# Sixteen transposes of the value tile moved from TensorE to the DMA, with a new start and a new order, in a fused scan and feed-forward kernel

## The chip, the cores and the metric

The kernel runs on one core of a Trainium2 chip. Times are device microseconds (us) of that core. A run is called slow when it takes over 1.5% more than the fastest run of the same kernel; ratios use the other runs ("fast runs") alone. The kernel before takes 269.89 us (median of 3 runs, 268.21 to 270.97).

## The reference, cut to what matters

```python
# r, k, v, w, a, b: [4 batches, 8 heads, 768 tokens, 40], float32
for t in range(S):
    y[:, :, t] = einsum('bhd,bhde->bhe', rt, state)
    Sa = einsum('bhde,bhe->bhd', state, at)
    state = state * wt[..., None, :] - einsum('bhd,bhe->bhde', Sa, bt)
    state = state + einsum('bhd,bhe->bhde', vt, kt)
x = y.transpose(0, 2, 1, 3).reshape(3072, 320)
out = maximum(x @ w_in, 0) ** 2 @ w_out        # w_in 320 x 2048, w_out 2048 x 320
```

A recurrence over 768 tokens in 32 independent heads gives `x`, and a feed-forward layer turns `x` into the output of 3072 rows of 320 floats.

## The kernel before

The scan is done in chunks of 64 tokens. Two batches at a time make a *group*: 12 chunks by 2 pairs of batches are 24 groups. Each group runs the recurrence of one chunk (KB, A, EB, XV, COR, ST) and the readout (CP, YC). Then its 128 rows go through the feed-forward layer (U, RL, SQ, D) and are stored (OE, OST). All operations of all groups stand in one long string, ORDER, which a search has produced; each engine is given its work in that order. `~10` in it means ten warm-up matmuls, whose result is not used.

Two parts matter here. The first is the value tile VM. After the correction (COR) two copies (MA, MB) finish VM; TensorE then transposes it in eight pieces (VT), VectorE copies the result out of PSUM (VTE), and CP reads it:

```python
def f():
    p = psum("vt", g, BF16)
    for i in range(8):
        nc.tensor.transpose(out=p[:, 128*i:128*i + 128], in_=vm[:, 128*i:128*i + 128], identity=ID[:])
add("VT", g, "PE", 0.447, f, [("MA", g), ("MB", g)], mode="M", alloc=("S", "vt"))
def f():
    nc.vector.tensor_copy(out=vmt[:], in_=psum("vt", g, BF16)[:])
add("VTE", g, "DVE", 0.692, f, [("VT", g), ("CP", g - 2)], frees="vt")
add("CP", g, "PE", 0.243, lambda: tri("cp", vmt, rh), [("VTE", g), ("RTE", g)], ...)
```

The second is the key tile KB. From group 6 on (`KDMA = 6`) it is transposed by one DMA already, issued on SP (KX), while groups 0 to 5 use TensorE (KT) and VectorE (KTE):

```python
nc.sync.dma_start_transpose(out=V(kbt, 0, [(128, 8), (1, 128)]), in_=kb[:])     # KX
```

The store of the group's result takes 128 partitions of 320 floats. Its rows lie in two batches of the output, and so its destination has an outermost dimension of 2:

```python
dst = out[b0 * T + c * L:b0 * T + c * L + L, :]
dst = bass.AP(dst.tensor, dst.offset, [[T * DM, 2], [DM, L], [1, DM]])   # 2 x 64 x 320
nc.sync.dma_start(out=dst, in_=osb[:])                                    # OST, once per group
```

Of the kernel before, what the change touches and what calls it, by code (L numbers as in the profile page):

```python
# [8 lines left out]
BF16 = mybir.dt.bfloat16  # L9
# [6 lines left out]
TBL.0 zK2.0 LWb.0 zL1.0 zR1.0 zS2.0 LWa.0 zV3.0 zR2.0 zU0.0 LKa.0 LWa.1 zA1.0 zS1.0 LKb.0 LWa.2 zF1.0 LBa.0 ones.0  # L16
zV1.0 UI.0 LAa.0 zF0.0 UE.0 LBb.0 ID.0 LWb.1 zL0.0 zF2.0 LN.0 LV1.0 SELB.0 LKb.1 TI.0 LO.0 zK0.0 LAb.0 zA0.0 zS0.0
LV0.0 ~10 CS.0 TE.0 LWb.2 zR0.0 EXN.0 I2.0 CE.0 LR.0 LAb.1 KBS1.0 KBS0.0 EXE.0 LAb.2 LN.1 zV0.0 ~3 KT.0 LR.1 LBa.1
AS.0 KTE.0 SEL.0 ~3 AT.0 wi1.0 LAa.1 MASK.0 LN.2 ATE.0 GLM.0 VC.0 LO.1 ~2 EB.0 LBb.1 EBE.0 LV0.1 ~1 CE.1 LKa.1 LO.2
EXE.1 zU1.0 LWb.3 ~1 XV.0 zK1.0 RT.0 LR.2 UB.0 zF3.0 LAa.2 LV1.1 UA.0 zV2.0 RTE.0 ~2 COR.0 wi2.0 CS.1 MA.0 LWa.3  # L20
CE.2 AS.1 MB.0 EXN.1 LKb.2 LV1.2 ~1 AT.1 VT.0 EXE.2 LAa.3 ATE.1 wj1.0 VTE.0 ST.0 KBS0.1 KBS1.1 CP.0 zR3.0 LBa.2
LV0.2 CPE.0 KT.1 LBb.2 wj2.0 LN.3 KTE.1 LKa.2 AS.2 ~2 CS.2 RT.1 EXN.2 STE.0 LAb.3 YC.0 wj0.0 RTE.1 EB.1 YE.0 LO.3
SX.0 VC.1 EBE.1 LKa.3 LR.3 CE.3 wi0.0 EXE.3 SXE.0 XV.1 LBa.3 LV1.3 wp0.0 AT.2 UA.1 RT.2 ATE.2 LKb.3 UB.1 KBS0.2 CS.3
wp1.0 RTE.2 COR.1 KBS1.2 LBb.3 XT.0 AS.3 MA.1 KT.2 XTE.0 MB.1 U1.0 wo0.0 KTE.2 EXN.3 VT.1 LV0.3 AT.3 VC.2 VTE.1 EB.2
UX1.0 GLM.1 GLM.2 EBE.2 UY1.0 LWb.4 ST.1 RL1.0 KBS0.3 LWa.4 STE.1 XV.2 X0.2 CP.1 LBb.4 UB.2 GLM.3 U0.0 CPE.1 KBS1.3
UA.2 UY0.0 LWa.5 UX0.0 wo1.0 KT.3 RL0.0 ATE.3 COR.2 KTE.3 YC.1 MA.2 YE.1 RT.3 MB.2 EB.3 SQ0.0 SX.1 RTE.3 LWb.5 XT.1
VT.2 XTE.1 LN.4 LKb.4 D0.0 EBE.3 VC.3 LO.4 ST.2 U0.1 LV0.4 SXE.1 CS.4 SQ1.0 D1.0 EXN.4 LAa.4 LBa.4 UX0.1 STE.2 LR.4
UY0.1 CE.4 VTE.2 RL0.1 LKa.4 XV.3 X0.3 CP.2 LWa.6 LN.5 U1.1 CPE.2 KBS1.4 UY1.1 EXE.4 LWa.7 UX1.1 UB.3 LAb.4 SX.2
LKb.5 RL1.1 SQ0.1 D2.0 LV1.4 SXE.2 D3.0 LWb.8 UA.3 LO.5 YC.2 OE.0 YS.2 LWb.6 KBS0.4 COR.3 YE.2 RT.4 LBa.7 D0.1 SQ1.1
RTE.4 LR.5 KT.4 LWb.7 MA.3 LV1.5 XT.2 D1.1 MB.3 XTE.2 AS.4 KTE.4 ST.3 LKa.5 VC.4 CS.5 LAb.5 U1.2 LBa.5 AT.4 LN.6  # L30
LAa.5 UX1.2 ATE.4 LBb.5 EXN.5 VT.3 LR.6 UY1.2 VTE.3 LV0.6 EB.4 RL1.2 OST.0 CE.5 EBE.4 LO.6 D2.1 LKa.7 EXE.5 LV0.5
RT.5 LN.7 STE.3 LBb.6 XV.4 KBS0.5 X0.4 U0.2 UB.4 CP.3 UA.4 D3.1 LAa.6 CPE.3 UX0.2 LKb.6 OE.1 KBS1.5 UY0.2 RTE.5
SQ1.2 SX.3 LAb.6 RL0.2 KT.5 LKa.6 SXE.3 CS.6 GLM.4 KTE.5 LBa.6 LO.7 COR.4 EXN.6 YC.3 SQ0.2 YS.3 LWa.8 AS.5 RT.6 MA.4
CS.7 YE.3 RTE.6 OST.1 D0.2 LV1.6 EXN.7 AT.5 XT.3 LWa.9 LV1.7 D1.2 ATE.5 VC.5 XTE.3 KBS1.6 EB.5 LKb.7 U0.3 MB.4 EBE.5
CE.6 LR.7 LWb.9 VT.4 LN.8 KBS0.6 D2.2 VTE.4 EXE.6 LBb.8 XV.5 LAa.7 X0.5 CP.4 UA.5 AS.6 D3.2 CPE.4 LBb.7 UB.5 UY0.3
OE.2 LO.8 KX.6 AT.6 VC.6 UX0.3 ATE.6 GLM.5 ST.4 LAb.7 RL0.3 YC.4 LKb.8 YS.4 LAb.8 COR.5 YE.4 CS.8 MA.5 LV1.8 U1.3
SQ0.3 LKa.9 MB.5 XT.4 UX1.3 KBS0.7 EXN.8 STE.4 UY1.3 VT.5 OST.2 LAa.8 RL1.3 XTE.4 D0.3 LWb.10 VTE.5 KBS1.7 EB.6
LBa.9 U0.4 SQ1.3 CE.7 LR.8 EBE.6 UY0.4 LN.9 LKb.9 UX0.4 EXE.7 LAb.9 D1.3 RL0.4 LWa.10 LO.9 SX.4 CP.5 SXE.4 GLM.6
ST.5 LV0.7 CPE.5 KX.7 RT.7 XV.6 AS.7 X0.6 D2.3 UA.6 SQ0.4 LV0.9 LKa.8 UB.6 D3.3 RTE.7 STE.5 U1.4 LR.9 LBa.8 CS.9
OE.3 LV1.9 COR.6 YC.5 MA.6 YS.5 LV0.8 UY1.4 YE.5 MB.6 UX1.4 KBS1.8 LKb.11 XT.5 SX.5 RL1.4 XTE.5 LKb.10 AT.7 SXE.5  # L40
CE.8 OST.3 SQ1.4 D0.4 EXE.8 VT.6 EXN.9 ATE.7 D1.4 LBb.9 LN.10 ST.6 VC.7 LO.10 LKa.11 U0.5 STE.6 EB.7 KBS0.8 LWb.11
UX0.5 EBE.7 D2.4 GLM.7 UY0.5 LAa.9 D3.4 VTE.6 RL0.5 KX.8 AS.8 RT.8 XV.7 LV0.10 X0.7 OE.4 SQ0.5 CP.6 U1.5 UA.7 OST.4
UY1.5 CPE.6 RTE.8 LWa.11 UX1.5 UB.7 AT.8 D0.5 RL1.5 ATE.8 SX.6 CS.10 SXE.6 LBb.12 YC.6 EXN.10 SQ1.5 COR.7 LWa.12
KBS0.9 YS.6 RT.9 MA.7 YE.6 D1.5 LWb.12 RTE.9 LAa.10 XT.6 D2.5 LBa.10 VC.8 XTE.6 KBS1.9 EB.8 MB.7 U0.6 EBE.8 LKa.10
LR.10 UY0.6 VT.7 GLM.8 LBb.10 LV1.10 UX0.6 VTE.7 D3.5 RL0.6 CE.9 KX.9 XV.8 OE.5 SQ0.6 X0.8 ST.7 EXE.9 CP.7 LN.11
STE.7 AS.9 OST.5 U1.6 UA.8 UY1.6 CPE.7 UB.8 LAb.10 UX1.6 LBb.11 D0.6 RL1.6 LO.11 AT.9 SX.7 ATE.9 LAb.11 LBa.11 CS.11
SQ1.6 LV1.11 YC.7 LWa.13 COR.8 YS.7 LV0.11 MA.8 D1.6 LWb.13 YE.7 MB.8 D2.6 LR.11 EXN.11 LWa.14 XT.7 KBS0.10 CE.10
XTE.7 VC.9 SXE.7 EB.9 U0.7 KBS1.10 EXE.10 EBE.9 ST.8 VC.10 VT.8 LAa.11 KX.10 UY0.7 LN.12 STE.8 D3.6 LV0.12 VTE.8
UX0.7 OE.6 AS.10 LWb.14 SX.8 RL0.7 RT.10 OST.6 SXE.8 LO.12 XV.9 X0.9 CP.8 UA.9 GLM.10 U1.7 LV1.12 CPE.8 RTE.10 UY1.7
UX1.7 LKb.14 UB.9 AT.10 RL1.7 LKb.12 CS.12 ATE.10 YC.8 SQ0.7 COR.9 LKa.12 KBS1.11 YS.8 RT.11 MA.9 YE.8 LBa.12 D0.7  # L50
EXN.12 KBS0.11 SQ1.7 XT.8 D1.7 MB.9 XTE.8 LAa.12 EB.10 LKb.13 VC.12 U0.8 EBE.10 GLM.9 UY0.8 LR.12 RTE.11 KX.11 UX0.8
CE.11 VT.9 LN.13 LBb.14 D2.7 VTE.9 EXE.11 LO.13 XV.10 RL0.8 LBb.13 X0.10 AS.11 ST.9 CP.9 STE.9 VC.11 U1.8 LAb.13
D3.7 UA.10 CPE.9 LAb.12 UY1.8 UB.10 SX.9 OE.7 LR.13 UX1.8 SQ0.8 OST.7 CS.13 RL1.8 LKa.14 SXE.9 YC.9 YS.9 COR.10
KBS1.12 LKa.13 YE.9 EXN.13 AT.11 D0.8 ATE.11 KBS0.12 MA.10 CE.12 XT.9 D1.8 LN.14 LAa.13 XTE.9 MB.10 SQ1.8 EB.11
LO.14 U0.9 EXE.12 UY0.9 EBE.11 KX.12 GLM.11 VT.10 LV1.13 UX0.9 LR.14 VTE.10 ST.10 LWa.15 AS.12 XV.11 STE.10 X0.11
LWa.16 CP.10 UB.11 D2.8 CPE.10 UA.11 AT.12 RL0.9 D3.8 LWb.15 COR.11 ATE.12 RT.12 LBa.13 MA.11 YC.10 YS.10 MB.11 U1.9
YE.10 CS.14 LKa.15 OE.8 SQ0.9 SX.10 EXN.14 OST.8 XT.10 UY1.9 XTE.10 UX1.9 LBa.15 VT.11 RL1.9 LBa.14 D0.9 KBS0.13
VTE.11 EB.12 LKa.16 U0.10 SQ1.9 LAa.14 CE.13 EBE.12 D1.9 LAb.14 EXE.13 LKb.15 UY0.10 LN.15 LV0.13 LWb.16 UX0.10
RTE.12 SXE.10 D2.9 KBS1.13 RL0.10 ST.11 AS.13 KX.13 XV.12 STE.11 X0.12 CP.11 UA.12 GLM.12 U1.10 LV0.15 CPE.11 D3.9
LBb.15 AT.13 LV1.14 OE.9 UY1.10 UB.12 ATE.13 UX1.10 OST.9 LO.15 SQ0.10 RT.13 RL1.10 COR.12 YC.11 LWb.18 YS.11  # L60
KBS0.14 CS.15 YE.11 RTE.13 D0.10 LWa.17 EXN.15 LAa.15 XT.11 SX.11 LBa.16 XTE.11 MA.12 KBS1.14 EB.13 U0.11 MB.12
EBE.13 CE.14 LV0.14 LWb.17 D1.10 LN.16 LAb.15 VT.12 SQ1.10 EXE.14 KX.14 UX0.11 VC.13 LO.16 VTE.12 UY0.11 LV1.15
D2.10 SXE.11 LKb.17 RL0.11 XV.13 AS.14 RT.14 LBb.16 ST.12 LR.15 X0.13 STE.12 U1.11 UA.13 CP.12 LR.16 UB.13 UY1.11
CPE.12 LV1.16 RTE.14 D3.10 UX1.11 OE.10 AT.14 SQ0.11 RL1.11 OST.10 YC.12 COR.13 ATE.14 KBS0.15 YS.12 LWa.18 CS.16
YE.12 MA.13 SX.12 LBb.17 LAa.16 SQ1.11 MB.13 CE.15 VC.15 LKb.16 LAb.16 VT.13 D0.11 VC.14 VTE.13 LV0.16 D1.11 EXE.15
SXE.12 XT.12 EXN.16 GLM.15 D2.11 XTE.12 AS.15 RT.15 U0.12 GLM.13 RTE.15 EB.14 KBS1.15 UY0.12 EBE.14 UX0.12 KX.15
AT.15 RL0.12 D3.11 XV.14 LBb.18 ST.13 OE.11 SQ0.12 X0.14 LN.17 OST.11 CP.13 U1.12 UA.14 LV1.17 CPE.13 D0.12 VC.16
UY1.12 LO.17 UB.14 UX1.12 LWa.19 ATE.15 LV0.17 STE.13 CS.17 RL1.12 LWb.20 YC.13 LR.17 YS.13 COR.14 LBa.17 YE.13
KBS0.16 D1.12 MA.14 LBa.18 XT.13 MB.14 CE.16 GLM.14 XTE.13 EXN.17 VT.14 LBa.19 EXE.16 ST.14 VTE.14 LN.18 U0.13 EB.15
SQ1.12 LR.18 UX0.13 LKa.17 LO.18 UY0.13 EBE.15 D2.12 LKb.18 RL0.13 KBS1.16 SX.13 STE.14 CP.14 LAb.17 KX.16 U1.13  # L70
CPE.14 XV.15 LV0.18 X0.15 RT.16 UA.15 D3.12 LAa.17 UB.15 SXE.13 UY1.13 RTE.16 LWb.19 AS.16 SQ0.13 COR.15 OE.12 YC.14
YS.14 LV1.18 MA.15 OST.12 CS.18 YE.14 UX1.13 MB.15 KBS0.17 AT.16 RL1.13 D0.13 ATE.16 LBb.19 KBS1.17 XT.14 SX.14
XTE.14 EXN.18 LKa.18 CE.17 ST.15 LWa.20 EXE.17 EB.16 AS.17 STE.15 U0.14 LWb.21 VT.15 SQ1.13 UX0.14 LKb.19 UY0.14
EBE.16 D1.13 RL0.14 SX.15 KX.17 D2.13 VTE.15 LN.19 D3.13 SXE.14 LR.19 LKb.20 XV.16 SXE.15 OE.13 LO.19 X0.16 RT.17
# [69 lines left out]
def kernel(  # L144
# [9 lines left out]
    moe_w_out: bass.AP,  # L154
    out: bass.AP,
):
    nc = tc.nc
    NB, NH, T, D = r.shape
    L = 64
    KDMA = 6  # L160
    AQ = 4
    NCH = T // L
    NG = NCH * (NB // 2)
    DFF = moe_w_in.shape[1]
    DM = moe_w_in.shape[0]

# [526 lines left out]
```

## Time and profile before

The profiled run of before took 264.9 us.

| engine | busy us | share |
|---|---|---|
| TensorE | 243.5 | 92% |
| VectorE | 180.1 | 68% |
| ScalarE | 163.2 | 62% |
| GpSimd | 162.3 | 61% |
| DMA (mean of 16 engines) | | 79% |

The prediction below shows and reads the lines of the page, the stretches and the chain of waits.

### The profile page before, as it was taken

What the parts mean: (1) busy time and instruction counts of PE and PEld (TensorE: products, weight loads), DVE (VectorE), ACT (ScalarE), POOL (GpSimd) and SP (SyncE); (2) the same over time, 40 slices, a digit from 0 to 9 for tenths busy, and PEclk for the clock granted to TensorE, in tenths of its full rate; (3) what the DMA queues carried; (4) which work ended last, traced back from release to release, by engine and by line L of the source; (5) the groups of instructions that cost most, each with busy time, mean ns of one, the idle gap of its engine ahead of it and who ended that gap; (6) DMA issues with size and microseconds to landing.
All of it is one profiled execution on the core that took longest, in us unless ns stands there. A gap on an engine that the chain in (4) does not pass through costs nothing.

```text
span 264.9 us, 13096 instructions
## 1 busy us (share of the span) xinstructions
PE 243.5 (92%) x5809; PEld 193.8 (73%) x5809; DVE 180.1 (68%) x296; ACT 163.2 (62%) x289; POOL 162.3 (61%) x244
## 2 busy tenths in 40 slices
PE   4887979999999999999999999999999899999970
PEld 1345767877877788787877788888878688878750
DVE  7659976696856676768666668686767658786520
ACT  2344665687755757775675876578485675646340
POOL 3789728987975469567489758576967593400000
PEclk9979999999999999999999999999999999999997
DMA  7999999798799699789699879779899677200110
GB/s 117 156 180 169 202 199 167 137 155 155 141 143 136 127 132 161 145 141 144 106 135 152 169 120 169 131 133 139 138 113 142 110 131 102 66 25 16 32 36 26
DMA packets 111913, 33.75 MB, mean 127 GB/s; under 512 B 101232, under 2 KB 109808, under 8 KB 111856
## 3 DMA queue, kind: packets, MB, share of 16 engines
q1 hardware_dynamic: 100272, 20.79, 52.0%
q0 software_dynamic: 9472, 11.80, 25.2%
q8 instruction: 45, 0.74, 1.2%
q10 hardware_dynamic: 2112, 0.33, 0.8%
q14 instruction: 12, 0.10, 0.1%
HBM read 28.84 MB, written 3.93 MB: 124 GB/s over the span
## 4 chain that ended last, share of the span: by engine, by line
PE 74%; DMA 5%; ACT 2%; issue 2%; POOL 1%; DVE 0%; ACTq 0%; POOLq 0%
PE fo L569 19%; PE hp L551 15%; DMA KBT<-KB 5%; PE hp L542 4%; PE vt L488 4%; PE sx L476 3%; PE eb L405 2%; PE cs L298 2%; PE x L420 2%; PE cp L405 2%; PE y L502 2%; PE ce L311 2%; PE rt L376 2%; PE st L457 2%; PE x L442 2%; PE ar L369 2%
## 5 line engine op out<-in xcount | busy, mean ns | idle before, releaser
L556 ACT ACTIVATE RL<-hp 128x1024 bf16<-128x1024 f32 x46 | 47.1, 1023 | 32.7 <-PE hp L551 32.2
L569 PE MATMUL fo<-WOUT,GT 128*128 128x320 bf16 x384 | 65.5, 300 | 0.6 <-DVE GT L560 0.5
L331 POOL TENSOR_TENSOR KB<-KBf,EXN 128x320 bf16<-128x320 f32 x45 | 40.6, 909 | 36.9 <-PE y L502 21.4
L551 PE MATMUL hp<-XT,WIN 128*128 128x128 bf16 x736 | 51.7, 219 | 1.1 <-issue 1.0
L551 PEld LDWEIGHTS <-WIN 128*128 128x128 bf16 x768 | 44.9, 98 | 4.8 <-issue 1.7
L560 DVE TENSOR_TENSOR GT<-RL 128x1024 bf16<-128x1024 bf16 x48 | 37.8, 787 | 9.0 <-ACT RL L556 8.9
L569 PEld LDWEIGHTS <-GT 128*128 128x128 bf16 x384 | 33.0, 98 | 11.9 <-DVE GT L560 1.1
L409 DVE TENSOR_TENSOR CPM<-cp,MASK 128x1024 bf16<-128x1024 f32 x24 | 29.3, 1220 | 8.5 <-PE cp L405 8.5
L409 DVE TENSOR_TENSOR EBM<-eb,MASK 128x1024 bf16<-128x1024 f32 x24 | 29.3, 1221 | 7.6 <-PE eb L405 7.4
L343 POOL DMA_DIRECT2D Vf<-in_v_dram x48 | 33.9, 706 | 0.0
L290 POOL TENSOR_TENSOR LLO<-LNW 128x320 bf16<-128x320 f32 x24 | 18.4, 767 | 19.5 <-ACT LNW L282 15.2
L264 POOL DMA_DIRECT2D Af<-in_a_dram x40 | 28.2, 706 | 0.4 <-issue 0.4
L433 ACT ACTIVATE UZ<-x 64x320 bf16<-64x320 f32 x48 | 20.7, 431 | 9.7 <-PE x L428 8.1
L337 POOL TENSOR_TENSOR A<-Af,EXE 128x320 bf16<-128x320 f32 x24 | 21.2, 882 | 6.8 <-ACT EXE L320 2.3
L447 ACT ACTIVATE VM<-x 64x320 bf16<-64x320 f32 x48 | 20.6, 430 | 7.6 <-PE x L442 6.8
L304 ACT ACTIVATE EXN<-cs 128x640 f32<-128x640 f32 x24 | 16.9, 702 | 10.4 <-PE cs L298 8.7
L468 DVE TENSOR_TENSOR STB<-st,GLM 128x640 bf16<-128x640 f32 x22 | 18.0, 818 | 7.7 <-PE st L462 7.1
L515 DVE TENSOR_TENSOR YB<-y,EXE 128x320 bf16<-128x320 f32 x24 | 11.8, 490 | 13.5 <-PE y L510 12.0
L492 DVE COPY VMT<-vt 128x1024 bf16<-128x1024 bf16 x24 | 16.5, 686 | 4.4 <-PE vt L488 4.3
L282 ACT ACTIVATE LNW<-Wf 128x320 f32<-128x320 f32 x24 | 11.2, 468 | 12.8 <-PE ce L315 7.0
L542 PE MATMUL hp<-XT,WIN 64*128 64x128 bf16 x368 | 18.1, 217 | 0.0
L347 ACT ACTIVATE VM<-Vf 128x640 bf16<-128x640 f32 x24 | 17.5, 732 | 0.3 <-DMA Vf<-in_v_dram 0.2
(90 smaller groups left out, 454.6 us busy)
## 6 DMA issues: line engine op xcount, KB each, us to landing
Wf<-in_w_dram SPq DMA_DIRECT2D x48, 80.0 KB
Vf<-in_v_dram POOLq DMA_DIRECT2D x48, 80.0 KB, 5.2
out_dram<-OSB SPq DMA_DIRECT2D x24, 160.0 KB
KBf<-in_k_dram SPq DMA_DIRECT2D x46, 80.0 KB
KBf<-in_b_dram SPq DMA_DIRECT2D x46, 80.0 KB
Af<-in_a_dram POOLq DMA_DIRECT2D x40, 80.0 KB, 4.6
RB<-in_r_dram POOLq DMA_DIRECT2D x24, 80.0 KB, 4.8
WOUT<-in_moe_w_out_dram POOLq DMA_DIRECT2D x2, 640.0 KB, 9.2
```

The lines of the kernel that those rows point to most:

```text
L264: q_.dma_start(out=V(dst, step * be, [(40, 8), (1, 40)], 64 * h, 64), in_=tok(src, b0 + be))
L331: (nc.vector if g < 3 and be else nc.gpsimd).tensor_tensor(out=V(kb, 512 * be, [(64, 8), (1, 40)]), in0=V(kbf, 320 * be, [(40, 8), (1, 40) ...
L337: nc.gpsimd.tensor_tensor(out=V(at, 0, [(64, 8), (1, 40)]), in0=V(af, 0, [(40, 8), (1, 40)]), in1=V(exe, 0, [(40, 8), (1, 40)]), op=ALU.mult)
L343: nc.gpsimd.dma_start(out=V(vf, 320 * be, [(40, 8), (1, 40)], 64 - 64 * be, 64), in_=tok(v, b0 + be))
L409: nc.vector.tensor_tensor(out=V(dst, 0, [(64, 16), (1, 64)]), in0=V(psum(key, g), 0, [(64, 16), (1, 64)]), in1=V(MASK, 0, [(0, 16), (1, 64 ...
L433: nc.scalar.activation(out=V(uz, 320 * be, [(1, 320)], 64 * be, 64), in_=V(psum("x", g), 0, [(1, 320)], 64 * be, 64), func=ACTF.Copy, scal ...
L447: nc.scalar.activation(out=V(vm, 512 * be, [(64, 8), (1, 40)], 64 * be, 64), in_=V(psum("x", g), 0, [(40, 8), (1, 40)], 64 * be, 64), func ...
L542: mm(out=V(p, 512 * s + 128 * i, [(1, 128)]), lhsT=wcol(1 + s, blk, 64 * s, 64), rhs=xt[64 * s:64 * s + 64, 128 + 128 * s:256 + 128 * s], ...
L551: mm(out=V(p, 512 * s + 128 * i, [(1, 128)]), lhsT=wcol(x, blk, 0, 128), rhs=xt[:, 128 * x:128 * x + 128], start=False, stop=i == 3 and x > 0)
L556: nc.scalar.activation(out=rl[:], in_=psum(hk, g)[:], func=ACTF.Relu)
L560: nc.vector.tensor_tensor(out=gt[:], in0=rl[:], in1=rl[:], op=ALU.mult)
L569: mm(out=p[:, 0:320], lhsT=gt[:, 512 * s + 128 * i:512 * s + 128 * i + 128], rhs=WOUT[:, DM * blk:DM * blk + DM], start=blk == 0, stop=blk ...
```

## The change

The intent is to take work from the busiest engine. In groups 6 to 21 one DMA transpose per group, issued on SP like KX, takes the place of eight TensorE transposes and a VectorE copy. The fill of `ones` and the other constants comes first at the start. The order was searched again for this program, with other assumed DMA times and 38 warm-up matmuls in place of 25. Those assumed times only feed the search; they don't enter the program.

```diff
+    VDMA = (6, 22)
...
-        def f():                       # VT and VTE in every group
+        if not VDMA[0] <= g < VDMA[1]:
+            ...                        # VT and VTE as before
+        else:
+            def f():
+                nc.sync.dma_start_transpose(out=V(vmt, 0, [(128, 8), (1, 128)]), in_=vm[:])
+            add("VX", g, "SP", 1.25, f, [("MA", g), ("MB", g), ("CP", g - 2)], dma=(102, 0.0092, 0.8, 1.0))
-        add("CP", g, "PE", 0.243, ..., [("VTE", g), ("RTE", g)], ...)
+        add("CP", g, "PE", 0.243, ..., [("VTE", g), ("VX", g), ("RTE", g)], ...)
...
-TBL.0 zK2.0 LWb.0 zL1.0 zR1.0 zS2.0 LWa.0 zV3.0 zR2.0 zU0.0 LKa.0 ...
+TBL.0 ones.0 LWb.0 zK2.0 UE.0 zR1.0 ID.0 zK0.0 LWa.0 zR0.0 zL0.0 ...
  (the whole ORDER is new)
```

## The prediction

> **What bounds the kernel now.** I read the page's first two parts, then the busy time by stretches, then the chain that ended last, then the groups of the instructions that the change touches, then the DMA queues. The page first: busy time by engine, then two rows of the span in 40 slices.
>
> ```profile
> PE 243.5 (92%) x5809; PEld 193.8 (73%) x5809; DVE 180.1 (68%) x296; ACT 163.2 (62%) x289; POOL 162.3 (61%) x244
> PE   4887979999999999999999999999999899999970
> DMA  7999999798799699789699879779899677200110
> ```
>
> TensorE is at 9 tenths from slice 7 to slice 37; no other engine reaches 70%. The DMA row is high too, in a different way: many small packets in flight. The stretches (busy us of each engine in each) say how much idle TensorE has to give back.
>
> ```profile
> core 0: us, PE busy (x) PEld busy (x) DVE busy (x) ACT busy (x) POOL busy (x), PEclk, DMA share, GB/s
> 0.00:10.00 10.00, 6.38 (x27) 2.17 (x27) 7.39 (x40) 2.90 (x5) 4.14 (x12) 1.00 0.81 127
> 20.00:30.00 10.00, 7.97 (x200) 5.91 (x197) 9.40 (x16) 5.94 (x13) 9.57 (x15) 1.00 1.19 181
> 140.00:160.00 20.00, 20.00 (x505) 16.43 (x500) 13.48 (x21) 15.29 (x27) 14.06 (x23) 1.00 0.89 147
> 200.00:220.00 20.00, 18.86 (x469) 15.18 (x468) 12.88 (x19) 13.03 (x23) 14.75 (x24) 1.00 0.81 130
> ```
>
> From 140 to 160 us TensorE has no gap at all; the worst full stretch, 200 to 220, has 1.1 us. Added over the nine stretches of 20 us from 40 to 220 us the gaps are 4.2 us (the wait for the other engines is nearly gone). The first 40 us are different: VectorE is at 94% and GpSimd at 96% from 20 to 30 us, and the DMA share is above 1. So there are two stages: a start of some 40 us that VectorE, GpSimd and the loads set, and a body of some 215 us that TensorE's instruction stream sets. Next the chain.
>
> ```profile
> PE 74%; DMA 5%; ACT 2%; issue 2%; POOL 1%; DVE 0%; ACTq 0%; POOLq 0%
> 133.45 6.13 DMA KBT<-KB
> 139.62 0.41 PE eb L405 x16
> ...
> 141.38 0.45 PE vt L488 x8
> ...
> 200.14 6.85 DMA KBT<-KB
> 207.03 0.41 PE eb L405 x16
> ```
>
> Columns of the pieces: start, us, what. Two things matter here. The eight transposes of VM (vt, L488) lie on the chain as pieces of about 0.45 us, up to 0.55 us. And the only other engine with a share is the DMA: twice the chain runs through the existing DMA transpose of KB, whose result came 6 to 7 us after its issue.
>
> ```profile
> L488 PE MATMUL vt<-ID,VM x192: 216/219/230, 20.1 to 243.5; 128*128 128x128 bf16 x192
> L492 DVE COPY VMT<-vt x24: 673/690/692, 20.7 to 243.8; 128x1024 bf16<-128x1024 bf16 x24
> L363 SPq DMA_TRANSPOSE KBT<-KB x18: 1251/1608/2970, 63.5 to 227.8; - x18
>   DMA KBT<-KB: 4.4, 5
> ```
>
> These are the groups of three lines (least, median and longest ns), and last, from the view of tile KBT, what readers of KBT waited for: 4.4 us in 5 waits (weight loads and matmuls). The 18 transposes that exist already cost TensorE little. They are the model for the 16 new ones, which have the same shape.
>
> ```profile
> q1 hardware_dynamic: 100272, 20.79, 52.0%
> q0 software_dynamic: 9472, 11.80, 25.2%
> ```
>
> Queue, packets, MB, share of 16 engines: together 77% of the span, and 80 to 100% in the body.
>
> [...] One transpose here lasts 219 ns, but they overlap: eight take 0.45 us in the chain, 56 ns each, and that is the cost to count. [...] the trace shows both queues busy at once. [...] the trace shows several us to landing[...].
>
> **The change part by part.** It removes, in groups 6 to 21: 16 x 8 = 128 transposes and as many weight loads on TensorE, and 16 VectorE copies. TensorE: 16 x 0.45 us = 7.2 us, and with the pieces that took up to 0.55 us, 8 us. I take 7.5. All of it lies in the body where TensorE has almost no gap, so it is on the path. VectorE: 16 x 0.69 = 11.0 us, at 68% busy and off the path; worth something only where TensorE waits for VectorE (EBM, CPM and GT), and each group needs one slot less of the three PSUM banks that small results share (eight users instead of nine). I put 1 us on both.
>
> It adds 16 DMA transposes on SP's queue. Issue: 16 x 1.6 us = 26 us on SP, which per group of about 10 us has six loads of 0.63 us, one transpose of 1.6 and one store of 0.6, or 6.0 us; it becomes 7.6 of 10. That fits, but SP takes its work in order. On the 16 DMA engines: the packet records of the trace show 18,432 packets of 256 bytes for the 18 transposes, 1,024 each, 656 us in sum, so 656/16/18 = 2.3 us per transpose on each engine, of which 64 x 18 ns (the median) = 1.15 us is undisturbed. So 16 x 1.15 to 2.3 = 18 to 37 us on each engine, within 160 us at a share of about 0.88: up to 1.0 or 1.1 (shares above 1 did occur at 20 to 40 us, at 180 to 200 GB/s, so the engines can do it, with longer landings).
>
> Does the new latency lie hidden? From the same packet records, matching each transpose's issue with its completion packets, the 18 landed after 2.4 to 7.2 us, mean 4.4. In the changed program's order I counted the TensorE work between the end of COR of a group (after which VM is evicted) and its CP (which reads VMT): 6.5 us on average, least 5.7, most 7.2, each block at its in-stream time (transposes x8 0.45, fo x4 0.54, hp x8 0.45). In the trace of before the same counting gives about 188 us for what took 213 us from 40 us on, so times 1.13: 7.3 us. The two evictions of VM take 0.9 us[...], which leaves 6 us for SP's queue and the landing. The mean of 4.4 fits; of the old landings three or four of 18 would not, by about 1 us each. With the busier queues I count 3 us of new waits in all, and 1 us more for KBT, whose room shrinks a little (from 6.4 to 5.5 us of TensorE work).
>
> The constants first: VectorE sets ones_b at 3.39 us now and GpSimd waits 3.1 us for it. That wait goes. But the first cs matmul, at 8.00 us, needs TI (a copy on VectorE that ended at 7.3) and LLO (6.7, after W's landing at 5.4). In the new order TI still stands behind some fifteen fills of VectorE, so it comes at about 7.2. The gain is 0 to 0.7 us there. The 13 added warm-up matmuls fill gaps. For the whole new start order I count 1 us.
>
> Sum: -7.5 - 1 + 3 + 1 - 1 = -5.5, taken as -6 for the search, which was made for this program with DMA times nearer to those in the trace: 269.9 - 6 = 263.9, say 264.0 us.
>
> **The rivals.** *(A) The wait takes the place of the work:* VMT comes late in most groups, so that CP waits 0.5 us each time, 16 x 0.5 = 8 us, and nothing is won: about 269. For it: two DMA transposes already cost the chain 6 to 7 us, and the share of the queues is near 1. Against it: only 4.4 us of waits in 18 transposes. *(B) The loads become the bound:* KBf and Wf land later because the engines are full, GpSimd gets its operands late, and everything shifts: 270 to 275. For it: GpSimd waited up to 5.0 us once for KBf. Against it: four buffers of each, filled some groups ahead. *(C) TensorE's stream shortens fully and the new order also cuts hidden waits* (the 1.13 above has some 25 us of short waits that the busy time hides): 257 to 260.
>
> **Range and chances.** The removed 7.5 us is the firm term; the waits may be 0 to 10 and the new order may give or take 3. That gives 258 to 269.5 eight times in ten. The line of 2% is at 264.5, close to my number: faster 0.52, same 0.43, slower 0.05.
>
> **What would show each step.** Right: 64 matmuls of vt instead of 192, 8 VMT copies, 34 SP transposes; TensorE's busy time down by about 7 us; DVE near 169 us; waits of cp for VMT by DMA of about 3 us and for KBT of about 5; the start no more than 2 us earlier. Wrong: waits for VMT of 8 us or more (A); GpSimd waiting over 20 us for KBf (B); TensorE's gaps as before and a span under 256 (C). If the TensorE blocks between two groups take longer in spite of fewer of them, the reason is one that I have not seen.

What no trace shows is cut: most of the paragraph before "The change part by part", and the time until the evictions of VM are seen, an estimate without a source (in after 8 of 16 VX are issued 0.02 to 0.03 us after the second eviction); without it the room is 7.3 - 0.9 = 6.4 us in place of 6. The sum lost no term by this: it came to -5.5, taken as -6, so 264.0 us. The longer landings at 20 to 40 us do stand in the trace of before: loads of Wf and KBf issued there landed after 7.5 us on average, those from 40 to 220 us after 5.5.

## The result, and the profile after

After takes 310.73 us (median of 4 runs, 307.57 to 314.10) where before took 269.05 us in the same rounds (4 runs, 267.29 to 270.97). A ratio is the mean time of one kernel's fast runs over that of the other's fast runs of the same rounds, so not quite the ratio of the medians: here 1.151 (1.136 to 1.166). The change makes the kernel 15% slower. The range on record ended at 269.5.

First the page of after: busy time by engine, the slices of TensorE, of the clock that TensorE was granted and of the DMA engines, and the two large DMA queues (packets, MB, share of 16 engines).

```profile
PE 259.1 (84%) x5694; PEld 200.3 (65%) x5694; DVE 168.1 (54%) x280; ACT 163.5 (53%) x289; POOL 161.1 (52%) x244
PE   7988787999593999839969698994999988699990
PEclk9999988999899699969969959998699999799996
DMA  8999995986949799899999999679989989960010
q1 hardware_dynamic: 117168, 24.98, 65.9%
q0 software_dynamic: 9472, 11.80, 23.5%
```

The work did move as planned: VectorE is 12 us less busy and TensorE runs 115 instructions fewer (128 transposes gone, 13 warm-ups added). But the row of TensorE, nearly all nines before, now has holes (3, 5, 6, 4) from slice 10 to the end, and the granted clock dips in the same slices or the next ones. TensorE is even *more* busy than before, 259.1 us against 243.5, since its instructions last longer: a matmul of the second feed-forward product went from 300 to 312 ns, one of the first from 219 to 233 ns, at a mean granted clock of 0.913 after 0.988. By the trace's clock record each of the seven waits of TensorE of 3.1 to 6.1 us is followed by a stretch at half the clock (0.50), which begins 1.9 to 4.9 us after the start of the wait; two more, at 37.9 and 51.5 us, come without so long a wait, and one at the very end. The span grew by 310.3 - 264.9 = 45.4 us. Of this, 29.8 us are idle time of TensorE (51.2 us after 21.4) and 15.6 us are longer busy time, although some 7 us of work had gone.

Next, stretches of 20 us (start:end, length, busy us of TensorE, weight loads, VectorE, ScalarE and GpSimd with their instructions, granted clock, DMA share, GB/s): one of before that the prediction doesn't show, and three of after.

```profile
40.00:60.00 20.00, 19.63 (x498) 15.96 (x493) 14.46 (x22) 13.82 (x26) 18.35 (x27) 1.00 0.88 151
```

```profile
40.00:60.00 20.00, 17.34 (x377) 14.08 (x376) 10.09 (x16) 10.22 (x17) 12.43 (x18) 0.88 1.00 151
80.00:100.00 20.00, 14.25 (x333) 11.28 (x333) 8.99 (x12) 9.03 (x16) 9.00 (x14) 0.90 0.82 128
200.00:220.00 20.00, 15.48 (x380) 12.83 (x376) 10.68 (x16) 10.28 (x19) 12.54 (x18) 0.88 1.00 127
```

Every engine is idle more. None has become the bound, though TensorE gets through 333 to 380 matmuls in 20 us where before did about 470 to 505. All are held by something else. The chain that ended last, and four of its pieces (start, us, what), say what:

```profile
PE 40%; DMA 38%; SPq 9%; issue 4%; POOL 3%; ACT 2%; DVE 1%; POOLq 0%; ACTq 0%; DVEq 0%
89.66 10.40 DMA VMT<-VM
100.10 0.61 PE cp L405 x16
...
124.54 12.43 DMA VMT<-VM
137.02 0.61 PE cp L405 x16
146.79 11.18 DMA KBT<-KB
```

The DMA's share of the chain went from 5% to 38%. A transpose of VM stands on the chain for 10 to 12 us from issue to landing. The prediction gave it 6 us of room. The old transposes of KB also land later, after up to 11 us. The list of waits (engine, line, releaser: us in total, times, longest):

```profile
ACT LNW L282 <- DMA Wf<-in_w_dram: 17.1, 7, 4.3
POOL KB L331 <- DMA KBf<-in_k_dram: 16.2, 8, 3.8
PE cp L405 <- DMA VMT<-VM: 15.4, 4, 6.1
PE eb L405 <- DMA KBT<-KB: 12.5, 5, 4.5
```

TensorE waits 15.4 + 12.5 = 27.9 us for transposes. Few waits, each long: the question is why a DMA takes 10 us.

**A closer look at one of them.** The completion records of a DMA show increments of its semaphore, which I read as one for each DMA engine that has done its share. Around 86 to 100 us they read:

```text
DMA (issued at, us)         increments at, us
store of OSB      86.32     87.32;  92.05, 92.16
store of OSB      88.22     89.19;  95.33, 95.48
load KBf<-in_b    88.83     13 from 91.06 to 91.60;  92.48, 95.77, 96.02
transpose of VM   89.66     15 from 98.06 to 98.83;  100.06
```

A load ends with 16 increments. A store shows three: one about 1 us after its issue, at 87.32 us before any of its packets had started (87.7 us), then two when data landed. The packet records agree: ahead of these increments of data stand packets of 4 bytes, two for a store and 16 for a load. So I read a store as the work of two engines of the sixteen. I had looked closely at the transposes and not at a store that the change doesn't touch.

The load between shows what follows: 14 of its 16 shares had landed by 92.48 us, and the last two came at 95.77 and 96.02, right after the second store ended at 95.48. By this reading it had to wait for the two engines that the stores held. The view of the DMA from 88.2 to 90.2 us of after shows those two engines working nearly alone (row of slices; packets; queue with packets, MB, share of 16 engines; the store issued in it):

```profile
DMA  1201011320000113300001114000000130091111
DMA packets 52, 0.08 MB, mean 41 GB/s; under 512 B 0, under 2 KB 51, under 8 KB 51
q1 hardware_dynamic: 51, 0.07, 13.0%
out_dram<-OSB SPq DMA_DIRECT2D x1, 160.0 KB
```

13% of sixteen engines are 2.1 engines. A store is 128 packets of 1,280 bytes, so 64 on each of the two engines at a median of 55 ns: 3.5 us in which these two do little else. The second store was issued 1.9 us after the first, and still exactly two store packets were in flight for nine tenths of the time. So I take it that both stores ran on the same two engines, one after the other, from 87.7 to 95.1 us.

The transpose of VM suffered more than the load. In the packet records 461 of its 1,024 packets of 256 bytes started by 95.0 us, nearly all from 93.5 us on. Then they stood still: from 95.0 to 96.0 us 16 to 18 of them were in flight and only 62 more started, and in the next half microsecond 431 did. The stores had ended at 95.1 us, and the two late shares of the load landed at 95.77 and 96.02. So this transpose didn't go on with fourteen engines while two caught up; it looks as if the packets of all engines waited for the slowest. Other transfers were late with it: of a load that GpSimd had issued at 90.39 us, three shares landed by 94.79 us and the other 13 only from 96.14 to 96.26.

**The sum that was missing.** In the packet records of before the 24 stores take 202 us in all, on two engines 101 us each. All other packets take 198 us on each engine if spread evenly. That is 101 + 198 = 299 us on two engines, 113% of the span of 264.9 us, where the other fourteen have 75%. (An estimate: packet times can overlap and include waiting, so over 100% is possible; the DMA share of before is 1.19 from 20 to 30 us. The records don't name the engine of a packet; that all stores use the same two is taken over from the pair of stores above.) By this estimate the two engines were full before the change.

### The profile page after: what moved, and what is told of

It is laid out like the page before. It is cut to its first block, busy times and chain, and to the rows that moved or that the text cites. A ratio compares the mean times of both kernels' runs of the same rounds, so it can differ in the third digit from the quotient of the medians.

```text
span 310.3 us, 12888 instructions
## 1 busy us (share of the span) xinstructions
PE 259.1 (84%) x5694; PEld 200.3 (65%) x5694; DVE 168.1 (54%) x280; ACT 163.5 (53%) x289; POOL 161.1 (52%) x244
## 3 DMA queue, kind: packets, MB, share of 16 engines
q10 hardware_dynamic: 2112, 0.33, 0.7%
## 4 chain that ended last, share of the span: by engine, by line
PE 40%; DMA 38%; SPq 9%; issue 4%; POOL 3%; ACT 2%; DVE 1%; POOLq 0%; ACTq 0%; DVEq 0%
DMA VMT<-VM 12%; PE fo L574 11%; DMA KBT<-KB 10%; SPq L264 8%; PE hp L556 8%; DMA KBf<-in_k_dram 7%; DMA Wf<-in_w_dram 4%; DMA Af<-in_a_dram 4%; PE hp L547 2%; PE cp L405 2%; DMA KBf<-in_b_dram 2%; PE x L442 2%; PE x L420 1%; PE rt L376 1%; PE y L507 1%
## 5 line engine op out<-in xcount | busy, mean ns | idle before, releaser
L574 PE MATMUL fo<-WOUT,GT 128*128 128x320 bf16 x384 | 67.8, 312 | 1.1 <-DVE GT L565 1.1
L556 PE MATMUL hp<-XT,WIN 128*128 128x128 bf16 x736 | 57.9, 233 | 0.0
L556 PEld LDWEIGHTS <-WIN 128*128 128x128 bf16 x768 | 49.5, 105 | 4.8 <-issue 1.7
L574 PEld LDWEIGHTS <-GT 128*128 128x128 bf16 x384 | 34.7, 101 | 14.5 <-DVE GT L565 1.6
L565 DVE TENSOR_TENSOR GT<-RL 128x1024 bf16<-128x1024 bf16 x48 | 36.7, 764 | 9.2 <-ACT RL L561 9.1
L405 PE MATMUL cp<-ART,VMT 40*128 40x64 bf16 x384 | 10.8, 201 | 15.6 <-DMA VMT<-VM 15.4
L282 ACT ACTIVATE LNW<-Wf 128x320 f32<-128x320 f32 x24 | 11.2, 467 | 22.7 <-DMA Wf<-in_w_dram 17.1
L405 PE MATMUL eb<-ART,KBT 40*128 40x64 bf16 x384 | 10.4, 197 | 12.8 <-DMA KBT<-KB 12.5
L405 PEld LDWEIGHTS <-VMT 40*128 40x128 bf16 x384 | 7.9, 101 | 18.2 <-DMA VMT<-VM 16.3
```

Of the source, the lines that this page charges most:

```text
L405: mm(out=V(p, 512 * al + 64 * i, [(1, 64)]), lhsT=V(lt, 128 * i, [(1, 128)], 64 * al, 40), rhs=rt(j, be, al), start=True, stop=True)
L556: mm(out=V(p, 512 * s + 128 * i, [(1, 128)]), lhsT=wcol(x, blk, 0, 128), rhs=xt[:, 128 * x:128 * x + 128], start=False, stop=i == 3 and x > 0)
L565: nc.vector.tensor_tensor(out=gt[:], in0=rl[:], in1=rl[:], op=ALU.mult)
L574: mm(out=p[:, 0:320], lhsT=gt[:, 512 * s + 128 * i:512 * s + 128 * i + 128], rhs=WOUT[:, DM * blk:DM * blk + DM], start=blk == 0, stop=blk ...
```

## The experiments

The theory after this look, **T**: the stores fill two engines (113% by the estimate); each DMA transpose must pass them and holds the other engines meanwhile, as the one above seemed to (62 packets started in 1 us), so it lands late, and the more transposes there are, the worse it gets. Rivals: **R1**, the new order is bad in itself; **R2**, a DMA transpose costs this much whatever the stores do; **R3**, it is SP's queue, which takes its work in order (in the trace of after none of its 206 issues overlaps another, and its 58 stores and transposes stand in ORDER's sequence), and not the engines. All experiment kernels gave the right output. The expectations were written with other names: T is theory S there, R1 is theory O, and R2, together with SP's queue, is theory L.

### 1. The transposes or the order

`neworder_vt` keeps the new order and puts VT and VTE back in all groups, where the room between them was chosen by me. `oldorder_vx` does the reverse: the order of before, with VX in the place of VT.

```diff
  neworder_vt, on after
-    VDMA = (6, 22)
+    VDMA = (24, 24)
     (ORDER: VX.g -> VT.g ~0.9 us before VTE.g, VTE.g ~1 us before CP.g, counted in TensorE work)
  oldorder_vx, on before
     (the VDMA code of after; ORDER: VT.g -> VX.g, VTE.g dropped, for g = 6..21)
```

> The changed kernel's order with the value tiles transposed on TensorE as before (VT and VTE put just before CP, VX dropped); stores as they were. Theory O (the order is to blame): 295 us or more. Theories S and L (the DMA transposes are to blame): 266 to 275 us, with TensorE's busy time near 243 us and clock above 0.97.

> The order of the kernel before, with the DMA transpose of VM where its TensorE transposes stood in groups 6 to 21 (VMT copies dropped); stores as they were. It leaves less TensorE work between the transpose and CP than the searched order. Theories S and L: 300 to 330 us. Theory O: 262 to 275 us.

Measured: neworder_vt 288.94 us (285.17 to 289.56), ratio to before 1.070; oldorder_vx 318.58 us (315.22 to 321.59), ratio 1.178. The first lies between the two expected ranges, so neither theory has it whole: both parts cost. The transposes alone, in an order not made for them, cost 49 us, with 39.8 us of waits of cp for VMT in 15 waits. The new order without them costs 20 us. With the transposes it costs another 22 us (310.7 after 288.9). This does not yet tell T from R2.

### 2. The store on all engines

The store is cut into its two batches, 64 partitions each, so that the outermost dimension is 64 on both sides. Nothing else changes.

```diff
-            dst = bass.AP(dst.tensor, dst.offset, [[T * DM, 2], [DM, L], [1, DM]])
-            nc.sync.dma_start(out=dst, in_=osb[:])
+            for h in range(2):
+                half = bass.AP(dst.tensor, dst.offset + h * T * DM, [[DM, L], [1, DM]])
+                nc.sync.dma_start(out=half, in_=osb[64 * h:64 * h + 64, :])
```

> The changed kernel with each output store issued as two stores of 64 rows, so that the outermost dimension is 64 and not 2. Theory S (the stores run on two of the 16 DMA engines, 128 packets of 1,280 bytes at some 55 ns or 3.5 us per store, and what follows on those two engines, the transposes above all, waits for them): the waits of cp and eb for VMT and KBT, 28 us now, fall under 8 us, and the time comes to 258 to 268 us. Theory L (16 more transposes are simply too much for the 16 engines and SP's queue): 300 us or more, since the bytes are the same and SP issues 24 more DMAs. Theory O (the new order is bad by itself): 300 us or more.

> The kernel before with the same split of the stores. Theory S: the stores delay the KBT transposes and loads there too, but there is room: 262 to 268 us, waits for KBT under 2 us instead of 4.4 us. Theory L and theory O: 269 us, or 1 to 2 us more for the extra issues.

Measured: after_split 268.82 us (267.11 to 274.20), ratio to before 0.999 (0.991 to 1.008); before_split **258.02 us** (257.59 to 259.90), ratio 0.963 (0.956 to 0.970). These few lines take 42 us off after and 11 us off before (the packets of before_split fit 16 short ones per half store, section 4), so most of the loss of the change, in its own order, was not in the transposes as such (against R2). The first lies at the upper edge of what was expected under T, the second below its range: the stores cost before more than I had thought. And before_split beats both kernels.

The page of after_split, its wait for VMT, then the page of before_split with its row of TensorE and its line of the store from the list of DMA issues (count, KB each, median us to landing):

```profile
PE 243.0 (91%) x5694; PEld 189.6 (71%) x5694; DVE 168.1 (63%) x280; ACT 163.1 (61%) x289; POOL 160.8 (60%) x244
PE cp L405 <- DMA VMT<-VM: 7.4, 7, 2.6
```

```profile
PE 241.0 (94%) x5809; PEld 193.0 (75%) x5809; DVE 180.1 (70%) x296; ACT 163.0 (64%) x289; POOL 162.4 (63%) x244
PE   4778989899999999999999999999999999999993
out_dram<-OSB SPq DMA_DIRECT2D x48, 80.0 KB, 3.2
```

TensorE's busy time in after_split is back at 243 us, and its clock at 0.981: the low clock came with the holes and not by itself. In before_split TensorE is at nine tenths from slice 8 on, and no matmul waits for KBT any more. Mean times from issue to the last increment, from the completion records:

| us from issue to landing | before | before_split | after | after_split |
|---|---|---|---|---|
| KBT transposes | 5.3 | 5.0 | 7.5 | 5.5 |
| VMT transposes | | | 6.7 | 5.2 |
| stores | 6.2 | 3.2 | 6.3 | 3.5 |
| loads of Wf and KBf | 5.6 | 4.6 | 5.7 | 5.0 |

The longest VMT landing fell from 12.4 to 6.8 us. In the new order the transposes gain 1.5 to 2.0 us and the loads 0.7, as T has it. In the order of before their mean hardly moves (5.3 to 5.0 us) and the loads gain more (5.6 to 4.6 us), so it is not shown that the 11 us there came by way of the transposes.

### 3. The two by two again, with the stores spread

> The changed kernel's order, value tiles transposed on TensorE, stores split over 16 engines: the fourth corner of the square with the changed kernel (310.7), after_split (268.8) and neworder_vt (288.9). If the new order is bad only because its stores come in pairs and hold two engines, 258 to 262 us, like before_split (258.0). If its start is bad as well (TensorE had issued some 110 matmuls fewer by 60 us in after_split), 263 to 272 us. The effect of the DMA transposes with the stores out of the way is after_split against this: theory S says within 4 us, theory L says after_split is slower by 5 us or more.

> The old order with the DMA transpose where the TensorE transposes stood, stores split: with oldorder_vx (318.6), the kernel before (269.4) and before_split (258.0) the square for the old order. Theory S: the 60 us lost to the transposes shrink to less than half, 265 to 285 us, the rest being the short distance to CP (1.3 to 5 us of TensorE work against a landing of some 4 us). Theory L: 300 us or more.

`oldorder_vxearly_split` issues VX right behind MB, as early as the data allows, and `oldorder_vxfew_split` uses VX only in the five groups 6, 11, 15, 17 and 20, where CP comes latest after MB:

```diff
  oldorder_vxearly_split (ORDER)          MB.g ... VX.g   ->   MB.g VX.g
  oldorder_vxfew_split
-        if not VDMA[0] <= g < VDMA[1]:
+        if g not in VDMA:              # VDMA = (6, 11, 15, 17, 20)
```

> The same with the DMA transpose issued directly behind the second eviction of VM, so that 2.2 to 6.3 us of TensorE work lie before CP; stores split. If the transposes as such cost little, this takes 7 us off TensorE's stream and gives 252 to 260 us; if waits for VMT eat it, 260 to 272 us, with more than 8 us of waits of cp for VMT.

> before_split with the DMA transpose of VM only in the five groups whose CP comes 6.1 us of TensorE work or more after the eviction (6, 11, 15, 17, 20), against all sixteen in oldorder_vxearly_split (2.2 to 6.3 us, 282.7). If the distance decides, waits of cp for VMT stay under 2 us and the time is 255 to 259 us, up to 2 us under before_split; if each transpose costs by its own load, 5/16 of the 25 us, so 264 to 268 us.

Median times (us), with the two-engine store and the split store:

| order | V transposes | store on two engines | store split |
|---|---|---|---|
| before's | all on TensorE | 267.1 to 269.4 (1) | **258.0** (0.963) |
| before's | 16 by DMA, in VT's place | 318.6 (1.178) | 297.3 (1.108) |
| before's | 16 by DMA, right behind MB | | 282.7 (no ratio: too few fast runs) |
| before's | 5 by DMA, in roomy groups | | 263.2 (0.986) |
| new | all on TensorE | 288.9 (1.070) | 271.4 (1.018) |
| new | 16 by DMA (after) | 310.7 (1.151) | 268.8 (0.999) |

In brackets stands the ratio to the runs of before on the same chip in the same rounds; where two kernels ran in different rounds, the ratios compare them better than the medians. The ranges of the four new times: neworder_vt_split 270.58 to 278.36 us, oldorder_vx_split 292.90 to 299.09, vxearly 274.78 to 287.19, vxfew 261.92 to 266.89.

Read the last two rows. In the new order the DMA transposes cost 22 us while the stores sit on two engines, and *save* some 3 to 5 us when they don't (2.6 us by the medians, which come from two chips; by the ratios 1.018 - 0.999 = 0.019 of 269 us, or 5 us; the intervals, 1.011 to 1.025 and 0.991 to 1.008, don't overlap). T had expected a difference of less than 4 us. In this order the sign of the change's main idea depends on a store that it doesn't touch. A better placing of VT than mine might take some of the saving back.

The rows of the old order say that room matters as well. There CP follows close on VT, and a transpose that lands after 5 us comes too late even with spread stores: cp still waits 30.2 us for VMT, in 12 waits. This is a miss of T, which expected 265 to 285 us for oldorder_vx_split, less than half of the 60 us that oldorder_vx stands above before_split; 297.3 leaves 39 of them. So with too little room most of the cost of the transposes stays whatever the stores do, as R2 has it. The longer room of vxearly gives back 15 us of the 39, and cp waits 20.3 us; that was a miss too (at most 272 us expected). Three of its four runs were slow (the fast one took 274.8 us), so take it as a direction only. The five roomy groups, with VX right behind MB as well, leave no wait for VMT at all. Even so that kernel stays 5 us above before_split; 4.7 us of this stand as waits for KBT:

```profile
PE eb L404 <- DMA KBT<-KB: 4.7, 2, 3.2
```

I had expected 255 to 259 us if only the distance to CP counted and 264 to 268 us if each transpose costs through its own load on the DMA. 263.2 us is between them, nearer to the second. An added transpose seems to delay the others, but one kernel doesn't settle that.

### 4. Engines or queue

`after_actq` issues the two-engine store from ScalarE, so that SP's queue holds only loads and transposes. `before_cols` cuts the store into two as before_split does, but by columns, so that each half still has the outer dimension 2: as many issues as in before_split, still on two engines.

```diff
  after_actq
-            nc.sync.dma_start(out=dst, in_=osb[:])
+            nc.scalar.dma_start(out=dst, in_=osb[:])
  before_cols
+            for h in range(2):
+                half = bass.AP(dst.tensor, dst.offset + 160 * h, [[T * DM, 2], [DM, L], [1, 160]])
+                nc.sync.dma_start(out=half, in_=osb[:, 160 * h:160 * h + 160])
```

> The changed kernel with its stores unsplit but issued from ScalarE's queue: still two engines, but another ring, so that the transposes and loads do not stand behind a store in the same ring, only beside it. If it is the place in the ring that hurts[...], 270 to 290 us. If it is the time of the two engines itself, 295 us or more, since their work is the same.

> The kernel before with each store split by columns into two of 160 columns: two issues per group as in before_split, but the outermost dimension stays 2, so two engines. If the spreading over 16 engines is what gained 11 us in before_split: 268 to 280 us here. If splitting alone did it: 256 to 262 us.

By the packet counts of the queues both kept two short packets per store, so by the reading above two engines. In after_actq the 24 stores moved 3,120 packets from SP's queue to ScalarE's (5,232 there after 2,112), 130 each: 128 rows and two short ones. In before_cols the 24 added stores bring 3,120 more (103,392 after 100,272), so 130 each again. In before_split the count rises by 720 alone (100,992), which is what 48 stores of 64 rows and 16 short ones come to.

Measured: after_actq 301.15 us (299.13 to 302.77), ratio 1.131. Another queue gives back 9.6 of the 42 us that the split gives back (5 us by the ratios), so a store's place in SP's queue is a small part at most. Its packet records show the same picture: at 86.5 to 88.5 us some 20 packets of a transpose are in flight and nearly none starts for 2 us. before_cols takes 273.83 us (270.57 to 276.44), ratio 1.019 (1.010 to 1.028), where before_split takes 258.0. Two issues on two engines are no help, two issues on sixteen are worth 11 us: it is the spreading that gains. One part of R3 stays open. To issue a transpose kept SP for 2.8 us on average in after, 2.4 in after_actq, 1.7 in after_split and 1.9 in before. So it looks as if the two busy engines hold up SP too, and with it the loads that come next in its queue. No run tells this from the wait at the engines; the split cures both.

### 5. The store without any DMA transposes

`before_kt` transposes KB on TensorE in all groups, so that no DMA transposes are left; `before_kt_split` has the split store as well.

```diff
-    KDMA = 6
+    KDMA = 24
     (ORDER: KX.g -> KT.g, KTE.g shortly before EB.g)
```

> The kernel before with all KB tiles transposed on TensorE, so with no DMA transpose at all; stores on two engines. TensorE's stream grows by 18 x 0.45 = 8 us. Taken with before_kt_split. If the stores hurt chiefly through the transposes[...], this and its split twin differ by under 4 us (against 11 us with the transposes), and both are at 262 to 270 us. If the stores hurt any DMA alike, they differ by 8 us or more and this is at 272 us or more.

> The twin of before_kt with the stores split over 16 engines: 261 to 268 us under either theory (before_split's 258 plus 8 us of TensorE work, less what waits it saves).

Measured: before_kt 276.20 us (274.52 to 278.05), before_kt_split 273.66 us (271.28 to 275.19). With 18 DMA transposes the split gains 11 us, without them 2.5 us, and 42 us with 34, so the cost of the two-engine store grows with the number of transposes, as T has it (the 34 stand in another order, though). But the pair proves less than it seems. Both times lie above what was expected of them, and TensorE is full in both, as one stretch of before_kt and the same of before_kt_split show:

```profile
60.00:100.00 40.00, 39.48 (x960) 32.95 (x960) 28.81 (x43) 25.71 (x47) 27.55 (x42) 1.00 0.63 116
60.00:100.00 40.00, 39.40 (x966) 32.31 (x965) 29.37 (x44) 26.63 (x48) 26.63 (x40) 1.00 0.62 114
```

The loads of Wf and KBf do land earlier with the split, after 4.3 us and not 5.6, but TensorE had about 0.5 us of idle time in these 40 us to gain from it. So without DMA transposes the stores delay the loads as well; TensorE just doesn't wait for them there.

### 6. More stores

If stores on two engines are the cause, more of them must hurt more. The first try repeated the store as it stands:

```diff
             nc.sync.dma_start(out=dst, in_=osb[:])
+            nc.sync.dma_start(out=dst, in_=osb[:])
```

> The kernel before with each output store issued twice to the same place: the transposes and the order unchanged, only the work of the two store engines doubled (another 64 packets of some 55 ns per store on each, 3.5 us, 24 times). Theory S: since spreading the stores gained 11 us, doubling them costs at least as much again: 285 to 330 us. If only the total traffic counts, 24 stores of 160 KB on 16 engines are some 0.5 us per group of DMA time and the result is 268 to 273 us.

The 0.5 us there is an estimate; 128 packets of 55 ns on 16 engines are 0.44 us.

> before_kt (no DMA transpose, stores on two engines, 276.2) with every store issued twice. If the store engines hurt through the transposes, doubling costs far less than the 104 us it cost beside 18 transposes: 278 to 300 us. If they slow every DMA alike, 330 us or more.

Measured: 372.47 us and 340.75 us. Both are flawed. The second store writes the bytes of the first; it waited for it, and it did so on SP, in front of all loads:

```profile
SPq L581 <- DMA out_dram<-OSB: 135.7, 24, 8.1
```

SP waited 135.7 us in 24 waits. These two kernels tell nothing of the engines. The second try writes other rows, those of two chunks (four groups) further on, which are overwritten by their own store later:

```diff
             nc.sync.dma_start(out=dst, in_=osb[:])
+            if g < NG - 4:
+                far = bass.AP(dst.tensor, dst.offset + 2 * L * DM, [[T * DM, 2], [DM, L], [1, DM]])
+                nc.sync.dma_start(out=far, in_=osb[:])
```

> The kernel before with an extra store per group (20 of 24 groups) of the same tile to rows that a later store overwrites, so that no store waits for its twin. The two store engines get another 3.5 us per group. If the time of these engines is what counts: 285 us or more. If the doubled runs were slow only through the wait on SP's queue: 269 to 274 us.

> The same without any DMA transpose (before_kt was 276.2). If the store engines hurt chiefly through the transposes, the loss against before_kt is less than half of before_extra's loss against the kernel before. If they slow every DMA alike, the two losses are about equal.

Measured: before_extra 318.86 us (315.38 to 325.05), ratio 1.182, so 51 us for 20 more stores. before_kt_extra has no ratio, since too few of its runs were fast; its median of 294.72 us (289.07 to 295.04) is 18.5 us above that of before_kt, its one fast run 12.9 us. The dose works in the direction of T, and with DMA transposes in the program it costs more than twice what it does without. But 13 to 18 us without any transpose is not small: stores on two engines delay the plain loads too once there are enough of them.

### 7. What the new order costs

With the stores spread, the new order with TensorE transposes is 13 us slower than the old one (271.4 against 258.0). Part of this may be my placing of VT and VTE in it. But after is also late early on: by 60 us it has issued 899 matmuls, 38 warm-ups among them, and before 1,053 with 25; with split stores the counts are 949 and 1,060. So the start was suspected. `oldstart_split` takes the operations of the first groups in the order of before and the rest in that of after. `before_split_const` takes only the "constants first" into the order of before.

```diff
  oldstart_split (on after_split)      ORDER up to D3.1 as in before, then the rest in after's order
  before_split_const (on before_split) ones, UI, UE, ID, TI, TE, MASK, SEL, SELB, I2 and the fills
                                       in after's sequence, all else in before's
```

> after_split (268.8) with the instructions up to the second group's last output product put in the old order, the rest in the new order. If the start is where the new order loses, 261 to 265 us, with some 1,060 matmuls issued by 60 us. If the body is, 267 to 270 us.

> before_split (258.0) with only the constants and fills in the new sequence (ones_b first on VectorE, then as in the changed kernel). By the prediction's step this gains 0 to 1 us: 257 to 258. If it is part of the slow start, 260 us or more.

Measured: oldstart_split 268.08 us (263.38 to 270.52), no ratio, since three of its four runs were slow. It decides nothing: the one fast run, 263.38 us, lies in the range expected if the start is the loss (261 to 265), and 3.7 us below the best of after_split; but the profiled run, a slow one, issued only 980 matmuls by 60 us where some 1,060 were expected. before_split_const took 260.50 us (259.51 to 262.96), ratio 0.978 (0.968 to 0.987). That is no gain of 0 to 1 us, as the prediction had it, but 2.5 us more than before_split (4 us by the ratios, whose intervals just overlap), and it meets what was expected of a part of the slow start, "260 us or more". What in the new order costs some 10 us stays open.

## Why the prediction was wrong

**The counts.** Right: 64 matmuls of vt are left, 34 transposes on SP, and VectorE fell to 168.1 us (169 on record).

**The step that failed** is the one that begins "On the 16 DMA engines". It averaged the packets over 16 engines and came to 18 to 37 us more on each, at a share of 0.88: tight but possible. The stores of two engines were in that mean. By the estimate above the share of those two was 113% already, which leaves no room. What the step gave as the new landings, "three or four of 18 would not" fit "by about 1 us each", became waits of TensorE of up to 6.1 us and landings of up to 12.4 us. The step just before it, the issue on SP, was too low with it: 16 x 1.6 = 26 us, 43 us in after, where the 18 old transposes rose from 34 to 51 us too; with spread stores they took 26 and 31. (A reading that was slightly off: by stretches of 20 us from 40 to 220 us the DMA share was 0.75 to 1.01, not 80 to 100%.)

**The landing times** were low from the start. The record says a mean of 4.4 us for the 18 transposes, taken from matched packets. The semaphore increments say 5.3 us, with a longest of 8.7, since they count up to the last of the 16. That is what a reader waits for: the transpose whose last increment came at 100.06 us let cp start at 100.10, though 15 had come by 98.83. Of the margin between 4.4 us and a room of 6 us, this takes more than half.

**The wait for VMT** was put at 3 us. It was 15.4 us, and 7.4 us with spread stores. So this term was too small by 4 us even where the engines were even. The wait for KBT was put at 5 us in all and was 12.5 us.

**TensorE's 7.5 us** are borne out: with spread stores in the new order, 251.6 us of busy time with TensorE transposes became 243.0 with DMA transposes, 8.6 us less at the same clock (0.980 and 0.981). The time fell by 3 to 5 us; the sum of the prediction with the measured wait is -7.5 - 1 + 7.4 = -1.1 us. So the mechanism was right in this order, once the stores are out of the way. In the order of before the same exchange lost time even then: 5 us with five transposes, 39 with sixteen in VT's place. What the sum missed is that in the run with holes in TensorE's work the clock was lower too (0.913 after 0.988): 15.6 us of the 45.4 are busy time that got longer.

**The start**, put at -1 us, went the other way: after was 154 matmuls behind at 60 us, of which the stores explain 50 (949 with them spread).

**The search's order**, put at about half a microsecond's gain, costs 13 us with TensorE transposes and spread stores (15 by the ratios), my placing of VT and VTE included. The cause is not found.

**The rivals.** A (a wait takes the place of the work) and B (the loads become the bound) were each given a fixed size, 8 us and a few us. Both happened, and at far larger sizes: GpSimd waited 16.2 us for KBf and ScalarE 17.1 us for Wf. The sentence for the unforeseen case, TensorE blocks that take longer in spite of fewer of them, is what came.

## What to carry to other kernels

Before moving work to the DMA, count the load of each engine and not the mean: here the store with an outermost dimension of 2 posted two increments of data and kept two packets in flight, and a load and a transpose with 16 increments landed only after it had ended (96.02 and 100.06 us after 95.48). Check how many increments each kind of DMA in the program posts, the untouched ones too; here a store split into two halves of 64 rows was worth 11 us (269 to 258) where the planned change lost 42. And take landing times from the last increment: the 18 transposes of before landed after 5.3 us by it, where matched packets had given 4.4.
